# Two attention layers on one core: a chunk split in pairs, urgent score tiles on VectorE, and a new plan

## The chip, the cores and the metric

The kernel runs on one core of one Trainium2 chip. The metric is device time in microseconds (us). Runs of one kernel scatter over several us; the state of every run told here is "fast", and the slower ones among the fast runs of a kernel tend to have the lower granted TensorE clock (for the kernel before, 1082.2 us on average at 1.000 and 1086.3 at 0.994; more below). A ratio is the mean time of one kernel's fast runs over the mean of the other kernel's fast runs of the same rounds, so it is not quite the ratio of the medians that are quoted.

## The reference, cut to what matters

Twice in a row, an attention block and a gated MLP block over 2048 tokens of 448 values; 16 heads of 28.

```python
def _A_ref(x, wqkv, wo):                       # 16 heads, head size 28
    qkv = ...                                  # x @ wqkv, split
    scores = jnp.einsum("bhqd,bhkd->bhqk", q, k) * (Dh ** -0.5)
    p = _softmax(scores, axis=-1)
    o = jnp.einsum("bhqk,bhkd->bhqd", p, v)
    return ... @ wo
def _B_ref(x, w1, w2, w3, w4):
    h = _gelu(_layernorm(x, axis=-1) @ w1)
    hs = ... @ w2                              # h shifted by one and two tokens, quarter by quarter
    x1 = x + hs
    return x1 + _gelu(_layernorm(x1, axis=-1) @ w3) @ w4
x = A_x
for _ in range(2):                             # written out in the original
    x = x + _A_ref(_layernorm(x, axis=-1), A_wqkv, A_wo)
    x = x + _B_ref(_layernorm(x, axis=-1), B_w1, B_w2, B_w3, B_w4)
```

## The kernel before

A planner written in Python runs when the kernel is built. It sends the generators of all tasks through a model of the five engines and fixes the order of instructions on each engine; only that order and the semaphores reach the chip. Queries go in chunks of four tiles of 128 rows, keys in 16 tiles. ScalarE takes exp of three or two blocks of 512 scores at a time out of PSUM (`ps` in the profile, which the kernel uses in banks of 512 columns) into the buffers `PT`; TensorE multiplies them with V. Some score tiles are computed on VectorE instead (buffers `PD`), by an eviction (an instruction that reads the bank, after which the planner gives it free) and four steps:

```python
        def d_chain(blk, ys, pd):                 # a score tile on VectorE, after its eviction d_first
            ...
            yield op("dve", 0.6, lambda e: e.scalar_tensor_tensor(out=q, in0=lo, ..., in1=lo, ...), reads=[("yd", w)], writes=[fk])
            yield op("dve", 0.6, lambda e: e.scalar_tensor_tensor(out=q, in0=q, ..., in1=lo, ...), reads=[("yd", w), fk], writes=[fk])
            yield op(DTS[0], DTS[1], lambda e: e.tensor_scalar(out=pdt, in0=q, ...), reads=[fk], writes=[("pd", s)])
            ...
            yield op("dve", 0.6, lambda e: e.scalar_tensor_tensor(out=pdt.bitcast(I16), in0=hi, ...), reads=[("yd", w), ("pd", s)], writes=[("pd", s)])
```

TensorE is given fillers, matmuls on an identity into any PSUM bank that is free, meant to keep its clock up.

```python
    def keep_pe_busy(self, until):
        ...
            for b in banks:
                if b not in self.dead:
                    continue
                ds = self.P.deps("pe", reads, [key(b)])
                if all(d.t_end + 0.2 <= t + 0.02 for d in ds.values()):   # free by the PLAN's clock
                    pick = b
                    break
```

The softmax sums of a finished chunk go through two small DMAs with a reciprocal on VectorE between them:

```python
                yield dma("sp", lambda e: e.dma_start(out=rT[0:4 * n, :], in_=ub[28:128:32, ui, 0:NW]), ..., t=1.9, iss=0.57)
                yield op("dve", 0.86, lambda e: e.reciprocal(out=rT[0:4 * n, :], in_=rT[0:4 * n, :]), reads=[("rT",)], writes=[("rT",)])
```

## Time and profile before

| kernel before | us |
|---|---|
| three runs, median (lowest to highest) | 1083.24 (1082.53 to 1085.25) |
| the profiled execution | 1085.21 (span 1083.5, granted clock 0.997) |
| to the first exp / first to last exp / after it | 22.35 / 1006.20 / 54.95 |
| of the middle: ScalarE busy / idle | 989.62 / 16.58 |

The prediction shows the lines that these come from. One more group of the page belongs to them, the exps: count, busy time, mean ns, then the idle time just before them and its main releaser. (In the lines ACT is ScalarE, DVE VectorE, PE TensorE, PEld its weight loads, POOL GpSimd and SP SyncE; L1329 is line 1329 of the kernel.)

```profile
L1329 ACT ACTIVATE PT<-ps 128x1536 bf16<-128x1536 f32 (+1 forms) x808 | 925.0, 1337 | 16.7 <-PE ps L1182 8.7
```

808 exps make up 925 us of a span of 1083.5. Whatever shortens the kernel has to take exps away, or idle time before them, or shorten start and tail.

### The profile page before, as it was taken

The numbers are of one execution on the slowest core, as the hardware profiler recorded it, in microseconds if no ns is written. First come the engines' busy times: TensorE is split into PE (matmuls) and PEld (weight loads), VectorE is DVE, ScalarE is ACT, GpSimd is POOL, SyncE is SP. The second block draws the span as 40 slices with busy tenths as digits, with TensorE's granted clock in tenths as the row PEclk, the third lists the DMA queues.
The fourth block names the chain that finished last, engine by engine and source line by source line (L and its number), as shares of the span: only waits on it lengthen the run. The fifth ranks groups of instructions, "written<-read, shape, count | busy, mean of one in ns | idle before, by whom it ended". The sixth has DMA issues, their size and how long they took to land.

```text
span 1083.5 us, 34577 instructions
## 1 busy us (share of the span) xinstructions
PE 1012.5 (93%) x15675; PEld 415.0 (38%) x15675; DVE 608.5 (56%) x1180; ACT 1020.6 (94%) x921; POOL 311.8 (29%) x494
## 2 busy tenths in 40 slices
PE   7999999889999999999998999898999999999998
PEld 3333443334333432234333433343333333444455
DVE  7866156984663226841778544464866714365342
ACT  5999999999999999999997999999999999999942
POOL 3243106401541024510354000102763300333121
PEclk9999999999999999999998999999999999999999
DMA  4547202102301042000311032414221110211000
GB/s 123 123 119 224 76 21 51 28 12 74 68 21 22 26 106 48 20 17 25 100 41 31 27 114 82 115 56 114 61 47 30 31 51 12 62 39 21 12 15 28
DMA packets 91847, 62.08 MB, mean 57 GB/s; under 512 B 64580, under 2 KB 81092, under 8 KB 91700
## 3 DMA queue, kind: packets, MB, share of 16 engines
q1 hardware_dynamic: 88324, 51.78, 18.5%
q0 software_dynamic: 3376, 8.09, 2.7%
q8 instruction: 123, 2.02, 0.8%
q14 instruction: 24, 0.20, 0.1%
HBM read 26.98 MB, written 15.71 MB: 39 GB/s over the span
## 4 chain that ended last, share of the span: by engine, by line
ACT 80%; PE 13%; DVE 5%; DMA 1%; issue 1%; POOL 0%; DVEq 0%; ACTq 0%
ACT PT L1329 73%; PE ps L731 8%; ACT h2T L1709 4%; PE ps L1182 3%; PE ps L722 2%; ACT fb L1583 1%; DMA rT<-ub 1%; ACT L1329 1%; ACT L1709 1%; DVE st L862 1%; DVE fb L1239 0%; PE ps L1750 0%; DVE yd L1223 0%; DVE xn L882 0%; DVE PD L1241 0%
## 5 line engine op out<-in xcount | busy, mean ns | idle before, releaser
L1329 ACT ACTIVATE PT<-ps 128x1536 bf16<-128x1536 f32 (+1 forms) x808 | 925.0, 1337 | 16.7 <-PE ps L1182 8.7
L1182 PE MATMUL ps<-qT,kT 32*128 32x512 bf16 (+1 forms) x2304 | 317.0, 361 | 34.0 <-ACT PT L1329 26.0
L722 PE MATMUL ps<-PT,vaug 128*32 128x512 bf16 (+1 forms) x2275 | 252.0, 361 | 0.5 <-DVE ub L1408 0.5
L1182 PEld LDWEIGHTS ps<-qT,kT 32*128 32x128 bf16 x2304 | 79.4, 91 | 316.1 <-ACT PT L1329 294.8
L1750 PE MATMUL ps<-ident 128*32 128x256 bf16 x3888 | 172.2, 276 | 8.0 <-DVE x1b L1640 2.2
L731 PE MATMUL ps<-xT,w 128*32 128x512 bf16 (+2 forms) x2240 | 172.3, 361 | 1.7 <-DVE hT L1563 0.8
L1750 PEld LDWEIGHTS ps<-ident 128*32 128x32 bf16 x3888 | 108.3, 97 | 41.2 <-issue 15.3
L1700 DVE CAST h2T<-ps 128x512 bf16<-128x512 f32 (+2 forms) x108 | 65.1, 603 | 80.1 <-PE ps L731 71.0
L731 PE MATMUL ps<-w,h2T 128*32 128x448 bf16 x1512 | 101.4, 355 | 9.0 <-ACT h2T L1709 8.9
L1434 POOL TENSOR_TENSOR otn<-ub,fb 128x512 bf16<-128x512 f32 (+1 forms) x31 | 38.7, 1247 | 240.4 <-DMA fb<-rscr 238.2
L722 PEld LDWEIGHTS ps<-PT,vaug 128*32 128x32 bf16 x2275 | 70.5, 94 | 94.0 <-issue 78.0
L731 PEld LDWEIGHTS ps<-xT,w 128*32 128x32 bf16 (+1 forms) x2240 | 61.2, 95 | 54.9 <-issue 27.5
L990 POOL TENSOR_TENSOR sq<-kT 128x512 bf16<-128x512 bf16 (+2 forms) x32 | 31.0, 970 | 91.7 <-DVE kT L1004 88.4
L731 PEld LDWEIGHTS ps<-w,h2T 128*32 128x32 bf16 x1512 | 39.5, 96 | 43.9 <-issue 14.7
L1581 POOL TENSOR_TENSOR fb<-hT 112x512 f32<-112x512 bf16 (+1 forms) x32 | 35.8, 1119 | 66.0 <-DVE hT L1563 62.9
L731 PE MATMUL ps<-xT,wq_pad 128*32 128x512 bf16 x512 | 44.9, 383 | 2.7 <-DVE qT L1037 1.3
L731 PE MATMUL ps<-xT,wk_pad 128*32 128x512 bf16 (+2 forms) x576 | 46.4, 362 | 0.0
L868 POOL TENSOR_SCALAR vpe<-mv 128x1 f32<-128x1 f32 (+2 forms) x21 | 5.1, 245 | 142.0 <-DVE mv L863 142.0
L731 PE MATMUL ps<-wv,xT 128*32 128x448 bf16 x512 | 44.0, 356 | 0.8 <-ACT vaug L1081 0.6
L1423 DVE RECIPROCAL rT<-rT 16x128 f32<-16x128 f32 (+1 forms) x31 | 29.1, 938 | 27.5 <-DMA rT<-ub 27.3
L1655 POOL TENSOR_TENSOR x_res<-x_res,x1b 128x448 f32<-128x448 f32 x32 | 38.9, 1218 | 17.2 <-DVE xn L882 17.2
L990 POOL TENSOR_TENSOR sq<-qT 128x512 bf16<-128x512 bf16 x28 | 30.0, 1075 | 40.4 <-DVE qT L1037 36.7
(155 smaller groups left out, 1080.8 us busy)
## 6 DMA issues: line engine op xcount, KB each, us to landing
fb<-rscr SPq DMA_DIRECT2D x28, 256.0 KB
uscr<-ub SPq DMA_DIRECT2D x24, 256.0 KB
ub<-uscr SPq DMA_DIRECT2D x24, 256.0 KB
xnd<-xn SPq DMA_DIRECT2D x28, 128.0 KB, 1.7
x_res<-in_A_x_dram POOLq DMA_DIRECT2D x16, 224.0 KB, 3.8
xd<-x_res SPq DMA_DIRECT2D x16, 224.0 KB, 2.5
x_res<-xd SPq DMA_DIRECT2D x16, 224.0 KB, 3.0
out_dram<-obf SPq DMA_DIRECT2D x16, 112.0 KB, 1.7
```

Of the source, the lines that this page charges most:

```text
L722: return lambda e: e.matmul(out=out, lhsT=lhsT, rhs=rhs, start=start, stop=stop, **kw)
L731: r.append(e.matmul(out=out[c:c + w, :], lhsT=lhsT[:, c:c + w], rhs=rhs, start=start, stop=stop, tile_position=(0, c)))
L990: return op("pool", 0.15 + NW * 0.0018, lambda e: e.tensor_tensor(out=sq[:, si, 0:NW], in0=src, in1=src, op=ALU.mult), reads=rk, writes=[( ...
L1182: yield op("pe", max(0.055, 0.22 / nc_ * NW / 512.0), lambda e, i=i, kc=kc, j=j, g=g, a=a, NW=NW, bank=bank: e.matmul(out=ps[:, bank, i * ...
L1329: yield op("act", 0.05 + n * w * 0.000833, lambda e, bk=bk, s0=s0, n=n, w=w: e.activation(out=PT[:, s0:s0 + n, 0:w], in_=ps[:, bk[0]:bk[0] ...
L1423: yield op("dve", 0.86, lambda e: e.reciprocal(out=rT[0:4 * n, :], in_=rT[0:4 * n, :]), reads=[("rT",)], writes=[("rT",)])
L1434: yield op("pool", 0.2 + NW * 0.0021, lambda e: e.tensor_tensor(out=otn[:, g, 0:NW], in0=u, in1=rb[:, 0:NW], op=ALU.mult), reads=[uk, fk], ...
L1581: yield op("pool", 0.2 + NW * 0.00165, lambda e: e.tensor_tensor(out=f, in0=z, in1=z, op=ALU.mult), reads=hk, writes=[fk])
L1655: yield op("pool", 1.2, lambda e: e.tensor_tensor(out=X, in0=X, in1=X1, op=ALU.add), reads=[xk, ("x1b", s)], writes=[xk], deps=[nop_])
L1700: ev = op("dve", c_ps(NW), lambda e, fch=fch, b=b: e.tensor_copy(out=hb[:, fch, 0:NW], in_=ps[:, bi(b), 0:NW]), reads=[("ps", bi(b))], wri ...
L1709: yield op("act", c_act(nl * NW), lambda e: e.activation(out=hb[:, 0:nl, 0:NW], in_=hb[:, 0:nl, 0:NW], func=ACT.Gelu_apprx_tanh), reads=al ...
L1750: return [e.matmul(out=ps[32 * c:32 * c + 32, bi(b), 0:256].rearrange("p (a n) -> p a n", n=128), lhsT=ident[:, 32 * c:32 * c + 32], rhs=i ...
```

## The change

Its intent: let the first layer's last query chunk run as two pairs of tiles, so that its MLP starts sooner; compute more score tiles on VectorE in all chunks; raise the priority of such a tile's steps when its use is near; transpose the last keys of layer 1 straight from SBUF instead of through DRAM; order the tasks by one rank list; keep fillers longer off a bank that VectorE is to free (0.7 us for 0.2); and let the planner make a new plan from all this. The diff, cut to its core (the planner's bookkeeping is made faster in it too, and its search constants are new):

```diff
-    CHUNKS = {0: [(0, 4), (4, 4), (8, 4), (12, 4)], 1: [(0, 4), (4, 4), (8, 4), (12, 2), (14, 2)]}
+CHUNKS = {0: [(0, 4), (4, 4), (8, 4), (12, 2), (14, 2)], 1: [(0, 4), (4, 4), (8, 4), (12, 2), (14, 2)]}
+RANK = {k: round(1.1 + 0.05 * i, 3) for i, k in enumerate([('a', 0, 0), ('k', 0, 1), ...])}
-D_RATE = {(0, 0): 0, (0, 1): 0.06, (0, 2): 0, (0, 3): 0, (1, 0): 0.045, (1, 1): 0.03, (1, 2): 0.015}
+D_RATE = {(0, 0): 0.08, (0, 1): 0.05, (0, 2): 0.05, (0, 3): 0.13, (1, 0): 0.16, (1, 1): 0.1, (1, 2): 0.16}
+Sched.AGED = 0.1
 Sched.TARGET = 0.64
-Sched.LOW = 0.34
+Sched.LOW = 0
-Sched.DOUBT = {"dma": 0.8, "pool": 0.6, "dve": 0.2, "act": 0.1}
+Sched.DOUBT = {"dma": 1.0, "pool": 0.4, "dve": 0.05, "act": 0.2}
 ...
-                if all(d.t_end + 0.2 <= t + 0.02 for d in ds.values()):
+                if all(d.t_end + (0.7 if d.eng == "dve" else 0.2) <= t + 0.02 for d in ds.values()):
 ...
+            if kc_of(1, t) >= FASTKV:                   # FASTKV = 3: key tiles 11 to 15 of layer 1
+                xslot[t] = s
+                yield ("sig", ("xns", t))
 ...
         def d_chain(blk, ys, pd):
+            def urge():
+                return 1.0 if at[0] > si or (at[0] == si and at[1] >= kb - DURG) else DPRIO
-            yield op("dve", 0.6, lambda e: ..., reads=[("yd", w)], writes=[fk])
+            yield op(DST[0][0], DST[0][1], lambda e: ..., reads=[("yd", w)], writes=[fk], urge=urge)
 ...
-                if rate and CHUNKS[L][ch][1] == 4:
+                if rate and CHUNKS[L][ch][1] == 4 and SC.idle_share(8.0) >= FTH:
```

## The prediction

No term of the sum is among the cuts: it stands at 1083.2 - 5.0 + 0.3 - 11.1 + 1.5 = 1068.9. The GpSimd instruction beside the 1630 ns step (588.36 us) is an addition (L1655, 587.85 to 589.43 us).

> **What bounds the kernel now.** I began with the page's busy line, then asked for windows that cut the span at the first exp (22.35 us) and at the end of the last one (1028.55 us), with narrower ones where ScalarE had gaps. Columns: window, length, then busy time and count of PE, weight loads, VectorE, ScalarE and GpSimd, granted clock, DMA share, GB/s.
>
> ```profile
> PE 1012.5 (93%) x15675; PEld 415.0 (38%) x15675; DVE 608.5 (56%) x1180; ACT 1020.6 (94%) x921; POOL 311.8 (29%) x494
> ```
> ```profile
> 0.00:22.35 22.35, 14.45 (x215) 6.97 (x215) 16.75 (x66) 10.13 (x16) 9.58 (x19) 1.00 0.46 137
> ...
> 200.00:235.00 35.00, 30.09 (x483) 12.61 (x484) 29.05 (x49) 33.08 (x29) 9.01 (x10) 1.00 0.15 22
> 235.00:530.00 295.00, 279.45 (x4189) 105.44 (x4181) 149.51 (x264) 294.64 (x253) 85.15 (x136) 1.00 0.19 46
> ...
> 570.00:600.00 30.00, 26.39 (x392) 10.77 (x392) 25.02 (x54) 22.23 (x22) 13.20 (x16) 0.89 0.21 41
> 600.00:740.00 140.00, 131.65 (x2071) 57.24 (x2068) 69.94 (x144) 139.85 (x120) 12.42 (x20) 1.00 0.28 83
> 740.00:760.00 20.00, 17.26 (x252) 6.32 (x251) 10.15 (x15) 17.48 (x16) 5.10 (x5) 1.00 0.40 85
> ...
> 1028.55:1083.50 54.95, 50.68 (x990) 32.09 (x987) 18.81 (x37) 20.83 (x36) 9.43 (x21) 1.00 0.07 21
> ```
>
> The kernel is three pieces in a row: 22.35 us of start, 1006.2 us in which ScalarE is busy 989.6, and a tail of 54.95 in which PE is busy 50.7. ScalarE bounds the middle: from 235 to 530 us it is idle 0.36 us in all. PE looks as busy, but 172 us of it are the filler matmuls on `ident`[...]. The middle's 16.6 us of ScalarE idleness are concentrated: 7.8 at 570 to 600, 2.5 at 740 to 760, 1.9 each at 200 to 235 and at 530 to 535.3, 0.8 at 800 to 860, 1.7 elsewhere.
>
> The waits of ScalarE and VectorE's own order of time (start, duration, line and operation) say what the largest gap is:
>
> ```profile
> ACT PT L1329 <- PE ps L1182: 8.7, 18, 1.5
> ...
> ACT PT L1329 <- PE ps L722: 7.3, 2, 5.8
> ```
> ```profile
> 588.36 1.63 DVE L1237 SCALAR_TENSOR_TENSOR fb<-yd 128x512 f32<-128x512 uint16 x1
> 589.91 0.41 DVE L1241 TENSOR_SCALAR PD<-fb 128x512 bf16<-128x512 f32 x1
> 590.25 0.67 DVE L1640 SCALAR_TENSOR_TENSOR x1b<-x_res,mst,ps 128x448 f32<-128x448 f32 x1
> ...
> 592.00 0.66 DVE L1244 SCALAR_TENSOR_TENSOR PD<-yd,PD 128x512 int16<-128x512 int16 x1
> ```
>
> L722 is the product with V. Two waits of ScalarE end with it, 7.3 us. Before the longer one, PE stands until VectorE finishes a score tile that VectorE was computing itself (PD, ready at 592.66); four other VectorE instructions were put ahead of its last step. PE takes its V products in order, the exp needs a P buffer that those free, and it restarts at 593.17. So VectorE, 56% busy over the span, stops ScalarE where it is crowded.
>
> [...] Here exps of 1536 and 1024 columns last 1548 and 1126 ns: 0.824 ns per column. [...] the L1237 step has a median of 687 ns and lasts 1630 beside a GpSimd product. [...] here a tile's 128 KB store to `xnd` lands in 1.7 us[...].
>
> **The change part by part.** I compared the instruction orders of the two programs.
>
> 1. *Score tiles on VectorE.* PD tiles go from 29 to 40: VectorE gains 11 chains, about 11 x 3.4 = 37.5 us busy (689+752+748+477+743 ns), while ScalarE has 2008 blocks of 512 columns left of 2019 (803 exps, not 808). The exps occupy 925.0 us for 2019 blocks, 0.458 us each; 11 less is **-5.0 us** on the bounding engine.
>
> 2. *Split of the last chunk.* An exp block of a two-tile chunk covers two key tiles, so it is still 512 columns and the exp count does not rise. Six 256-wide score matmuls took 0.32 us, as three 512-wide did. V products become 512 of 256 columns for 256 of 512, at about 0.045 and 0.055 us: +9 us on PE, beside a stretch of some 117 us in which the old order holds roughly 14 us of fillers. On ScalarE, four tanh of 512 become eight of 256; from start to start they take 0.52 and 0.30 us: 8 x 0.30 - 4 x 0.52 = **+0.3 us**. Table switches stay seven pairs. The gain sought is that the first 12 to 13 tiles reach their MLP sooner and the crowd at the layer boundary is spread.
>
> 3. *Urgent score chains.* They ran at lowest priority; now a chain rises when the scores come within one key block of it. That aims at the two L722 waits (7.3 us) and partly at the score waits around 214 to 220. From the order of VectorE's instructions, with durations from the rows, I summed the work between evictions of successive V accumulators. Before, one 28-block segment of layer 1 (12.8 us of exp) carries 19.5 us of VectorE work: the 585 us stall. In the new order the fullest 28-block segment there carries 11.5 us, the fullest 64-block one 26.1 in 29.3. No segment after the start is overfull[...].
>
> 4. *Keys straight from SBUF.* For key tiles 11 to 15 of layer 1 a store (1.7 us) and a transposed load (5.1) give way to a transpose of 2.5: 4.3 us less latency. But from 600 to 740 us, where those keys are made, ScalarE idles 0.15 us. Directly worth **0**; it moves the point of need, nothing more.
>
> 5. *New plan* (rank list, larger allowances for DMA latency, no forced fillers). It may remove the 2.5 us at 740 to 760, where the chain runs through the DMA of the reciprocal into the output projection ahead of score matmuls. It may also bring waits of its own. Of the old 16.6 us I let 5.5 remain: some 7 of the 7.3 and 4 of the other 9.3 go, **-11.1 us**. This is judgement, the term I trust least.
>
> 6. *Start and tail.* First exps follow nearly the same work, one more V eviction on an idle ScalarE: 0. After the last scores, the new tail has 56 plain 256-wide matmuls for 40 (20 took 2.34 us: +1.9) and 40 col-tiled 512-wide for 56 (40 took 2.33: -0.9). Between the last V product and the output projection stand only fillers where before there was real work, but it is made up later: +0.5. **+1.5 us**.
>
> Sum: 1083.2 - 5.0 + 0.3 - 11.1 + 1.5 = 1068.9; I say 1068.5.
>
> **The rivals.** (a) *VectorE becomes the bound.* For it: 37.5 us more there, eleven PD tiles crowded in layer 1's third chunk (24 us of chain beside other work)[...]. Against: 56% busy, no overfull segment, chains now urgent. If it wins, 10 to 16 us of idleness remain: 1073 to 1079. (b) *PE order becomes the bound at the boundary.* In windows of 32 blocks the new order, like the old, has a few holding 1 to 2 us more PE work than ScalarE work (around blocks 896 and 1120); equal in number and size to before, so perhaps 2 us: 1071. (c) *Only the smaller exp count counts*, because each removed stall uncovers one behind it: -5 + 0.3 + 1.5 and 1 or 2 us of stalls, 1078 to 1080. Against: ScalarE runs hundreds of microseconds without a gap, so a removed stall is not refilled by a second resource. (d) *Everything works*: no idleness in the middle, 1083.2 - 5.0 + 0.3 - 16.6 + 1.5 = 1063.4; to go below, the tail would have to shrink too, whose PE work of about 50 us bounds it.
>
> **Range and chances.** 2% faster is 1061.6 us, below (d): it needs every stall gone and a tail 2 us better than I count. I give that 0.07. Slower by 2% (1105) needs new waits of 35 us, 0.01. Range 1063 to 1077: from no stalls to rival (a).
>
> **What would show it.** Exps x803 and about 920 us of exp time; ScalarE busy in the middle near 985; the wait of exps on L722's successor below 1 us; idleness between first and last exp about 5.5 us; tail near 56.5. Wrong if the exps wait on V products again (a), if the score waits exceed 9 us (b), or if the last exp ends less than 8 us earlier.

## More of the kernel before

The experiments ran in four groups of rounds, each group on another chip, so versions of different groups are compared by their ratios to the kernel before.

A filler waits for the last reader of its bank: the page of the kernel before has 8.0 us of idle time in front of fillers (L1750), 2.2 of it for the eviction `x1b`.

## The result, and the profile after

| | before | after |
|---|---|---|
| median of 4 runs (lowest to highest) | 1082.88 (1082.15 to 1085.25) | 1080.91 (1080.21 to 1082.57) |
| ratio, 95% interval | | 0.998, 0.9961 to 1.0000 |
| profiled execution: time / span | 1085.21 / 1083.5 | 1080.76 / 1079.0 |
| start / middle / tail | 22.35 / 1006.20 / 54.95 | 21.83 / 1002.82 / 54.35 |
| middle: ScalarE busy / idle | 989.62 / 16.58 | 984.97 / 17.85 |

The time is 12.4 us above the prediction and outside its range. The interval reaches 1, so these four runs alone hardly show a gain; the control below does. First the page's busy line of the changed kernel and its row of exps; then the windows of the three pieces, with columns as in the prediction.

```profile
PE 1009.5 (94%) x16117; PEld 426.2 (39%) x16117; DVE 642.3 (60%) x1250; ACT 1016.7 (94%) x922; POOL 315.8 (29%) x503
...
L1367 ACT ACTIVATE PT<-ps 128x1536 bf16<-128x1536 f32 (+1 forms) x803 | 918.8, 1338 | 17.6 <-PE ps L1212 16.8
```
```profile
0.00:21.83 21.83, 13.80 (x215) 6.85 (x215) 16.80 (x66) 10.67 (x16) 9.58 (x19) 1.00 0.48 140
21.83:1024.65 1002.82, 944.75 (x14942) 388.10 (x14941) 606.88 (x1146) 984.97 (x869) 294.36 (x460) 0.99 0.23 58
1024.65:1079.00 54.35, 50.96 (x966) 31.25 (x961) 18.61 (x39) 21.07 (x37) 11.84 (x25) 1.00 0.10 26
```

The work on ScalarE shrank as foreseen: 803 exps, 984.97 us busy in the middle, 4.65 less. The idle time before the exps did not shrink: 17.6 us for 16.7. The releaser changed, though. The waits of ScalarE for the score matmuls and the V product, in the changed kernel:

```profile
ACT PT L1367 <- PE ps L1212: 16.8, 15, 3.9
```

The wait on the V product (7.3 us before) has no line any more. The wait for scores went from 8.7 us in 18 pieces of at most 1.5 to 16.8 us in 15 pieces of up to 3.9. Four windows hold 11.9 of the 17.85 us of idleness (ScalarE's busy time is the fourth one after the length; the three numbers at the end are granted clock, DMA share and GB/s):

```profile
102.00:116.00 14.00, 11.45 (x149) 4.09 (x152) 5.69 (x9) 10.94 (x10) 3.32 (x4) 0.88 0.69 230
331.00:345.00 14.00, 12.08 (x188) 5.24 (x180) 13.52 (x22) 11.63 (x11) 8.94 (x10) 0.88 0.19 46
560.00:576.00 16.00, 15.37 (x185) 6.19 (x181) 9.94 (x20) 12.11 (x13) 5.17 (x6) 1.00 0.44 107
807.00:822.00 15.00, 12.56 (x147) 3.56 (x136) 8.59 (x16) 12.44 (x12) 6.21 (x7) 0.89 0.18 28
```

That is 3.06, 2.37, 3.89 and 2.56 us; a fifth, at 765 to 772 us, holds 1.5. A sixth went unnoticed in the experiments:

```profile
32.18 2.37 ACT L1367 ACTIVATE PT<-ps 128x1536 bf16<-128x1536 f32 x2 [2.00 <-PE ps L1212]
```

The kernel before waits 0.48 us at this place (31.18 us). The 2.0 us stand in every version of the changed kernel that was traced here, the repaired ones too, and their cause was not tested.

What ends each of the five, read in order of time (start, duration, engine, line, operation, and in brackets the idle time before it and its releaser):

The wait at 107 to 115 us:

```profile
102.25 0.71 SPq L1460 DMA_DIRECT2D rT<-ub  x1
...
108.62 0.94 DVE L1461 RECIPROCAL rT<-rT 16x128 f32<-16x128 f32 x1 [2.75 <-DMA rT<-ub]
109.49 0.62 DVE L1084 TENSOR_TENSOR qT<-qT,ps 128x512 bf16<-128x512 bf16 x1
...
110.17 1.03 PE L1783 MATMUL ps<-ident 128*32 128x256 bf16 x16 [2.17 <-DVE qT L1084]
...
111.78 1.45 ACT L1367 ACTIVATE PT<-ps 128x1536 bf16<-128x1536 f32 x1 [2.51 <-PE ps L1212]
```

No exp needs this reciprocal. But the eviction of a PSUM bank (L1084) stands behind it on VectorE: the matmuls that it reads ended at 106.42 us, and it started at 109.49, as the reciprocal ended. A filler on TensorE waited 2.17 us for that eviction, and the score matmuls stand behind the filler. So an 8 KB transfer stops ScalarE through two queues (the experiments test this chain). It took 6.4 us from issue to the reciprocal. The same transfer later, with a DMA share of 0.02, takes 1.7:

```profile
724.57 0.55 SPq L1460 DMA_DIRECT2D rT<-ub  x1
...
726.31 0.94 DVE L1461 RECIPROCAL rT<-rT 16x128 f32<-16x128 f32 x1 [1.77 <-DMA rT<-ub]
```

From 100 to 109 us the DMA engines were full with two weight loads that GpSimd had just issued, as the DMA view of that stretch says (packets, MB and share of the engines' time; then KB and us to landing of the larger load):

```profile
q0 software_dynamic: 534, 2.85, 97.3%
...
w<-in_B_w_dram POOLq DMA_DIRECT2D x1, 1568.0 KB, 12.0
```

This kind of wait is not new. In the kernel before, a reciprocal starts at 752.22 us after 5.63 us of waiting for the same kind of transfer, evictions of `qT` stand behind it, and ScalarE loses 1.48 us just after. There the transfer took 5.8 us with a DMA share of 0.38 and no such weight load. So a late reciprocal is seen with full engines (97.3%) and without them; what delays the transfer was not tested.

The wait at 337 to 344 us has another cause and the same last link, a filler:

```profile
337.05 1.64 DVE L1281 SCALAR_TENSOR_TENSOR PD<-yd,PD 128x512 int16<-128x512 int16 x1
338.61 1.26 DVE L1673 SCALAR_TENSOR_TENSOR x1b<-x_res,mst,ps 128x448 f32<-128x448 f32 x2
339.34 1.47 PE L1783 MATMUL ps<-ident 128*32 128x256 bf16 x24 [1.84 <-DVE x1b L1673]
...
341.40 1.45 ACT L1367 ACTIVATE PT<-ps 128x1536 bf16<-128x1536 f32 x1 [2.12 <-PE ps L1212]
```

The last step of a score tile on VectorE takes 1.64 us beside a GpSimd product (L1472, 336.69 to 338.14 us) instead of 0.69 (the median of its 40), and the eviction `x1b` stands behind it. At 814 to 820 us the w3 projection stands ahead of score matmuls and waits for its transposed input, issued at 809.88:

```profile
809.88 1.22 SPq L901 DMA_TRANSPOSE xT<-xn  x1
...
815.75 0.51 PE L745 MATMUL ps<-xT,w 128*32 128x384 bf16 x8 [1.77 <-DMA xT<-xn]
```

At 765 to 772 us it is the w1 projection in the same way. At 569 us no engine waits for a DMA at the time: TensorE is busy, with the q projections of layer 1's second chunk, which the next scores need.

### The profile page after: what moved, and what is told of

The parts are those of the page before. It is cut to its first block, busy times and chain, and to the rows that moved or that the text cites. A ratio compares the mean times of both kernels' runs of the same rounds, so it can differ in the third digit from the quotient of the medians.

```text
span 1079.0 us, 35560 instructions
## 1 busy us (share of the span) xinstructions
PE 1009.5 (94%) x16117; PEld 426.2 (39%) x16117; DVE 642.3 (60%) x1250; ACT 1016.7 (94%) x922; POOL 315.8 (29%) x503
## 4 chain that ended last, share of the span: by engine, by line
ACT 72%; PE 18%; DVE 6%; DMA 3%; issue 1%; POOL 1%; SPq 0%; DVEq 0%; ACTq 0%
ACT PT L1367 65%; PE ps L745 9%; PE ps L1212 4%; PE ps L736 4%; ACT h2T L1742 3%; ACT fb L1616 1%; DMA rT<-ub 1%; PE ps L1783 1%; ACT L1742 1%; DMA xT<-xn 1%; ACT L1367 1%; DVE st L876 1%; DMA fb<-rscr 0%; DVE rT L1461 0%; DVE hT L1596 0%
## 5 line engine op out<-in xcount | busy, mean ns | idle before, releaser
L1367 ACT ACTIVATE PT<-ps 128x1536 bf16<-128x1536 f32 (+1 forms) x803 | 918.8, 1338 | 17.6 <-PE ps L1212 16.8
L736 PE MATMUL ps<-PT,vaug 128*32 128x512 bf16 (+1 forms) x2520 | 250.7, 341 | 0.2 <-DVE ub L1446 0.2
L745 PE MATMUL ps<-xT,w 128*32 128x512 bf16 (+2 forms) x2176 | 165.0, 362 | 5.3 <-DMA xT<-xn 3.2
L1783 PEld LDWEIGHTS ps<-ident 128*32 128x32 bf16 x3860 | 110.7, 97 | 38.0 <-issue 13.2
L736 PEld LDWEIGHTS ps<-PT,vaug 128*32 128x32 bf16 x2520 | 74.8, 95 | 92.8 <-issue 79.3
L1472 POOL TENSOR_TENSOR otn<-ub,fb 128x512 bf16<-128x512 f32 (+1 forms) x36 | 42.1, 1169 | 150.8 <-DMA fb<-rscr 150.5
L1614 POOL TENSOR_TENSOR fb<-hT 112x512 f32<-112x512 bf16 (+1 forms) x36 | 38.6, 1074 | 71.6 <-DVE hT L1596 54.7
L745 PE MATMUL ps<-xT,wk_pad 128*32 128x512 bf16 (+2 forms) x576 | 48.8, 359 | 0.4 <-DVE qT L1058 0.4
L1461 DVE RECIPROCAL rT<-rT 16x128 f32<-16x128 f32 (+1 forms) x36 | 33.6, 934 | 22.2 <-DMA rT<-ub 22.1
L1253 DVE TENSOR_SCALAR yd<-ps 128x512 int32<-128x512 f32 x40 | 27.2, 685 | 31.4 <-PE ps L1212 30.8
L745 PE MATMUL ps<-wv,xT 128*32 128x448 bf16 x512 | 41.2, 356 | 1.2 <-DVE kmaxc L1036 0.8
```

The costliest lines, as they stand in the source:

```text
L736: return lambda e: e.matmul(out=out, lhsT=lhsT, rhs=rhs, start=start, stop=stop, **kw)
L745: r.append(e.matmul(out=out[c:c + w, :], lhsT=lhsT[:, c:c + w], rhs=rhs, start=start, stop=stop, tile_position=(0, c)))
L1367: yield op("act", 0.06 + n * w * 0.000833, lambda e, bk=bk, s0=s0, n=n, w=w: e.activation(out=PT[:, s0:s0 + n, 0:w], in_=ps[:, bk[0]:bk[0] ...
L1472: yield op("pool", 0.2 + NW * 0.0021, lambda e: e.tensor_tensor(out=otn[:, g, 0:NW], in0=u, in1=rb[:, 0:NW], op=ALU.mult), reads=[uk, fk], ...
L1614: yield op("pool", 0.2 + NW * 0.00165, lambda e: e.tensor_tensor(out=f, in0=z, in1=z, op=ALU.mult), reads=hk, writes=[fk])
L1783: return [e.matmul(out=ps[32 * c:32 * c + 32, bi(b), 0:256].rearrange("p (a n) -> p a n", n=128), lhsT=ident[:, 32 * c:32 * c + 32], rhs=i ...
```

## The experiments

The theory, called "own waits" in the expectations: the new order took the old waits away, and brought about five of its own; each has its own cause and gives its time back when mended. Rivals: "refill" (a second resource bounds the middle, and a removed wait opens another), too many tiles on VectorE, the split, and the luck of the plan.

Most experiments edit the finished order and nothing else (some also drop fillers): no task planned anew, no wait taken away. A helper records each instruction's function, reads and writes, moves the listed ones, and then derives all semaphores anew from reads and writes in the new order, so that a moved instruction still waits for what it needs. The numbers are positions in the plan.

```diff
+    def rearranged(self, moves, drops):
+        order = [op for i, op in enumerate(self.all) if i not in drops]
+        ...                                   # take out the listed ops, put them before or after a given one
+        Q, new = Plan(), {}
+        for op in order:
+            eng, fn, reads, writes, deps, dma, t_end = op.args
+            new[id(op)] = q = Q.add(eng, fn, reads, writes, [new[id(d)] for d in deps], dma, t_end)
+        return Q
 ...
         est = SC.run()
+        P = P.rearranged(MOVES, DROPS)
         P.finalize(nc, st)
```

**Control.** `MOVES = []`, `DROPS = []` on the changed kernel.

> A control for the repairs: the changed kernel with its order taken apart and put together again by the same helper, with nothing moved and nothing dropped. All theories: the changed kernel's time, 1079.5 to 1082.5 us, ratio to the kernel before 0.996 to 1.000, and its five waits in their places (about 3 us at 107 to 115, 2.4 at 337 to 344, 3.9 at 569, 1.5 at 766 to 771, 2.5 at 814 to 820). If it is faster than 1077 by itself, the repairs prove nothing.

Measured: 1081.25 us (1080.12 to 1083.08), ratio 0.9974 (0.9960 to 0.9989). The helper does nothing by itself, and the changed kernel's gain over the kernel before is about 3 us on this chip. In its profile the waits stand at 110 (3.1 us), 340 (2.4) and 569 (3.9); those at 768 and 815 are 4.3 and 1.2 here instead of 1.5 and 2.6, so these two waits vary from execution to execution.

**The reciprocal alone.**

```diff
+MOVES = [([1007, 1013], 'after', 1016)]     # reciprocal and its store behind two qT evictions
```

> The changed kernel with one repair: at 102 us the reciprocal that waits for its DMA, and the store of its result, go behind the next two VectorE instructions of the q projection; nothing else moves. Theory 'own waits' (the new order has some five waits of its own, each with its own cause, and each gives its time back when mended): ScalarE's 3.06 us of idleness from 107 to 115 us falls below 0.8, and the time is 1080.9 - 2.5 = about 1078.4. Rival 'refill' (some second resource bounds the middle, a removed wait opens another): the wait at 107 to 115 goes but the time stays within 0.7 us of 1080.9, with the idleness found later. Rival 'the DMA itself': the exps depend on that reciprocal, and the wait stays at about 3 us in place.

Measured: 1077.40 us (1074.57 to 1079.27), ratio 0.9941 (0.9923 to 0.9960), which by ratio is 3.6 us below the control (0.0033 of 1084; the control is of another group of rounds, on another chip). The window that lost 3.06 us, in this run:

```profile
102.00:116.00 14.00, 13.42 (x206) 5.60 (x207) 8.21 (x13) 14.00 (x14) 3.40 (x4) 1.00 0.70 232
```

ScalarE is busy 14.00 of 14.00, and the clock in it is 1.00 instead of 0.88. The DMA is as busy as it was (0.70 for 0.69); only nothing stands behind it any more. The rival "the DMA itself" falls. Not all of the 3.6 us need be this repair: in the same profile the wait at 340 is 1.3 us, with nothing moved there.

**Two others alone**, `x1b` and w3:

```diff
+MOVES = [([3231], 'after', 3246), ([3227], 'after', 3237),   # x1b evictions ahead of the tile's last two steps
+         ([8206, 8207, 8211], 'before', 8225)]               # w3 matmuls behind two rounds of scores
```

> Two of the four repairs alone: the evictions of x1b ahead of the score tile's last steps at 331 to 338 us, and the w3 projection behind score matmuls at 812 us; the reciprocal at 102 us and the order at 768 us stay as in the changed kernel. Theory 'own waits': only the waits at 337 to 344 and 814 to 820 go, 2.4 + 2.5 us, and the others stay: 1080.9 - 4.5 = about 1076.5. Rival 'the first wait sets all' (mending the reciprocal shifted everything after it, and the other repairs gave nothing): 1080 or more.

Measured: 1076.45 us (1075.30 to 1077.44), ratio 0.9927 (0.9912 to 0.9941): as expected, and by ratio 5.1 us below the control of the same rounds. The idleness at 340 and 815 is gone from the profile; the waits at 110 (3.1 us by its window) and 569 (3.9) are still there.

**All four**, with the w1 projection at 768 us:

```diff
+MOVES = [([1007, 1013], 'after', 1016), ([3231], 'after', 3246), ([3227], 'after', 3237),
+         ([7784, 7785, 7789, 7794, 7795], 'after', 7801),    # a w1 group behind scores
+         ([8206, 8207, 8211], 'before', 8225)]
```

> The changed kernel with four repairs of the order: the reciprocal at 102 us; at 331 to 338 us two evictions (x1b) ahead of the last two steps of a VectorE score tile; at 768 us the w1 projection behind the score matmuls; at 812 us the w3 projection behind them. Theory 'own waits': 3.06 + 2.37 + 1.45 + 2.56 = 9.4 us of ScalarE idleness are aimed at, 7.5 to 9 come back: 1072 to 1073.5, idleness of the middle 9 to 10 us instead of 17.9. Rival 'refill': above 1078. Rival 'too many VectorE tiles': the wait at 337 to 344 stays, since VectorE is overfull there, and only some 6 us come back, about 1075.

Measured: **1072.46 us** (1071.72 to 1073.04), ratio 0.9898 (0.9882 to 0.9914). This version beats both kernels (the changed one by ratio, across groups of rounds). Its waits for scores, and its middle:

```profile
ACT PT L1387 <- PE ps L1232: 9.3, 9, 3.9
```
```profile
21.90:1016.47 994.57, 940.18 (x14940) 387.49 (x14941) 606.40 (x1146) 984.15 (x869) 293.73 (x460) 1.00 0.23 58
```

Idleness of the middle 10.4 us instead of 17.85, with the same work on ScalarE. So three of the new waits were separable, and neither "refill" nor "too many tiles" explains them. The fourth repair gave nothing: the wait at 768 us is 1.6 us here, for the next w1 group now stood ahead of the scores and waited for the eviction that I had moved back. What is left besides is mainly the 3.9 us at 569 and the 2.0 at 32.

**The old waits, mended in the kernel before.** Were the 7.3 us that the change removed worth 7.3 us?

```diff
+MOVES = [([4909], 'after', 4875), ([4914, 4916, ..., 4928], 'after', 4903),    # tile's last step, V products
+         ([5446, 5453], 'after', 5438), ([5476, ..., 5491], 'after', 5444), ([5501, 5503, 5504], 'before', 5492)]
+DROPS = [5456, ..., 5471]                                                      # 16 fillers
```

> The kernel before with its two waits for a VectorE score tile mended by order alone: the last step of the tile goes ahead of other VectorE work at 531 and at 589 us, the V products go ahead on TensorE, and 16 fillers in between are dropped. No score tile more, no split. If the waits that the change removed are worth what I put them at, 5 to 7 us come back from 1083: 1076 to 1078, ratio about 0.994 to 0.995, and the two waits of exps on the V product fall from 7.3 to below 1.5 us. Rival 'refill': 1081 or more, the idleness reappearing within the next 30 us as waits for scores.

Measured: 1084.79 us (1083.64 to 1086.84), ratio 1.0013 (0.9998 to 1.0027): nothing came back. The waits on the V product fell from 7.3 to 1.6 us, and those for scores rose from 8.7 to 11.8. In order of time:

```profile
592.09 1.23 DVE L1261 TENSOR_SCALAR PD<-fb 128x512 bf16<-128x512 f32 x1
...
593.50 0.68 DVE L1428 COPY ub<-ps 128x512 f32<-128x512 f32 x1
...
594.24 0.80 PE L742 MATMUL ps<-PT,vaug 128*32 128x512 bf16 x6 [2.71 <-DVE ub L1428]
...
595.62 1.02 ACT L1349 ACTIVATE PT<-ps 128x1024 bf16<-128x1024 f32 x1 [3.53 <-PE ps L1202]
```

VectorE, busy 9.83 of the 10 us from 585 to 595, now holds up the eviction of the V accumulator (`ub`) instead of the score tile. A second try put that eviction ahead of two more steps of a tile:

```diff
+         ([5475, 5490], 'after', 5498)])
```

> The earlier repair of the kernel before gave nothing back (1084.8 for 1083.9): the wait for the VectorE tile at 589 us turned into a wait for the eviction of the V accumulator, VectorE being busy 9.8 of the 10 us from 585 to 595. Here that eviction goes ahead of two more steps of a score tile too. Theory 'VectorE is overfull there': a third wait follows, and at most 2 us come back, 1082 to 1084. Rival 'only the order was wrong': 5 us come back, 1078 to 1079.

Measured: 1084.21 us (1080.80 to 1086.97), ratio 1.0002 (0.9980 to 1.0024). The profiled execution was the fastest of its four, with 5.7 us of idleness left between 580 and 600. Here "refill" fits: in the old kernel VectorE is overfull for some 10 us, and both orders tried only moved the wait about. In the changed kernel work has left that stretch: VectorE is busy 20.65 us from 570 to 600, for 25.02 before.

**The wait at 569 us.** The q projections there need tile 7, stored 20 us earlier by the plan; their load waits for one of two `xT` buffers, which the w1 projection of tiles 12 and 13 holds from 520 to 550 us of the plan.

```diff
+         ([5766, 5772, 5779, 5789], 'after', 5727), ([5799], 'after', 5729),    # last w1 quarter earlier
+         ([5796], 'after', 5728),                                               # then the load
+         ([q projections..., w3 groups...], 'refill', None),                    # q first in the slots of both
+         ([7805], 'after', 7808)]
+DROPS = [5855, 5856, 5857, 5862]
```

> The four repairs plus two: the last quarter of the w1 projection of the tiles 12 and 13 goes ahead on TensorE (it held one of the two xT buffers from 520 to 550 us of the plan, so that the load for layer 1's second q projection waited), that load and its four q projections go ahead of the w3 projection, whole groups swapped, four fillers dropped; and at 768 us one more w1 group goes behind the score matmuls. Theory 'own waits, the one at 569 us caused by a buffer that the split's small chunk holds': the 3.9 us at 569 fall below 1, and about 0.7 more at 768: 1072.5 - 4 = 1068 to 1069, idleness of the middle about 7.5 us. Rival 'refill' (TensorE is full at the layer boundary, the w3 projection and the later keys come late in turn): above 1071, with waits for scores between 575 and 620.

Measured: 1074.58 us (1073.28 to 1078.92), ratio 0.9910 (0.9891 to 0.9929): not below the four repairs, where 1068 to 1069 was expected. The wait is still 3.6 us; the load came 5.0 us earlier (554.96 and 549.94 us in the two traces, 6.0 counted from the first exp), but the scores stood behind the w3 groups that I had put after the q projections. So once more, with those groups moved behind the scores, one at a time:

```diff
+         ([5809, 5810, 5813, 5814, 5819], 'after', 5915), ([5816, ..., 5823], 'after', 5926),
+         ([5828, ..., 5836], 'after', 5938), ([5845, ..., 5854], 'after', 5945)]
```

> As the run with the two more repairs, but the four w3 groups that gave way to the q projections now go behind the first score matmuls of the new chunk, one group at a time between later score matmuls, instead of ahead of them. Before this run: [...] the wait at 565 us was still 3.6 us, TensorE busy 5.0 of every 5 us from 540 to 565 with no filler to give way. Theory 'only the order': the wait falls below 1.5 us and the time is 1070 to 1071.5. Rival 'TensorE is full at the boundary' (it has some 5 us of fillers in the 120 us from 530 to 650): the w3 groups push the later work, the same 3 us come back as waits for scores between 570 and 620, and the time stays at 1072.5 to 1074.5.

Measured: 1075.87 us (1074.53 to 1079.69), ratio 0.9926 (0.9906 to 0.9947), above what either theory expected. Two windows of its profile:

```profile
565.00:570.00 5.00, 3.83 (x43) 1.35 (x36) 2.72 (x6) 3.97 (x4) 1.51 (x2) 1.00 0.16 56
570.00:575.00 5.00, 3.75 (x30) 1.76 (x29) 2.51 (x6) 2.70 (x4) 0.00 (x0) 1.00 0.53 105
```

The 3.9 us are now 5.3 in several pieces from 560 to 580. My theory of the held buffer falls as the sole cause. But "TensorE is full" isn't shown either: it is busy 3.8 of 5 us in these windows, waiting about half a microsecond at a time, mostly for VectorE to evict the w3 groups' results (`h2T`). What bounds this boundary stays open; I found no order that mends it.

**Single parts of the change**, planned anew, so each of these also draws a new plan, and one of them shows how far a draw alone can move the time:

```diff
-FASTKV = 3
+FASTKV = 9                       # keys never straight from SBUF
```

> The changed kernel without the keys transposed straight from SBUF (all keys by the store and the transposed load, as before); the planner then makes nearly the same plan (same 803 exps, 40 VectorE tiles, same lateness of the q projection at 569 us). My prediction put this part at 0: within 1.5 us of the changed kernel, 1079.4 to 1082.4. If the fast keys are what brought the waits at 768 and 814 us (more transposes on the queue), the run is 2 to 4 us faster than the changed kernel; if they saved time, 2 us or more slower.

Measured: 1084.54 us (1079.59 to 1089.09), ratio 1.0009 (0.9986 to 1.0032). Above the 1079.4 to 1082.4 that I expected and some 3 us slower by ratio than the changed kernel, as foreseen for the case that the part saves time; but the six runs spread over 9.5 us (granted clock 0.997 in the fastest, 0.991 in the slowest). The waits at 110, 340, 569 and 815 are all in its profile, so the fast keys did not bring them. Whether the part is worth 3 us, or this plan only has more places where TensorE's clock falls (it is 0.66 from 1020 to 1035 us in the profile, which is of the slowest run), isn't settled.

```diff
-CHUNKS = {0: [(0, 4), (4, 4), (8, 4), (12, 2), (14, 2)], ...
+CHUNKS = {0: [(0, 4), (4, 4), (8, 4), (12, 4)], ...      # and ORDER and BGROUPS to match
```

> The changed kernel with its first layer's last chunk left whole (four tiles), everything else of the change kept; the planner then makes 50 VectorE tiles and 799 exps. If the split is what brought the wait at 569 us (a small chunk holding an xT buffer), that wait is gone here. What the split was meant for should show in its place: the keys of layer 1's last tiles, or another product of the last chunk's MLP, come late, and one wait of 10 to 22 us appears between 660 and 720. Expected 1083 to 1093, slower than the changed kernel by 2 to 12 us; if the split is worth nothing, 1076 or less, since 4 exps fewer are worth 4 us.

Measured: 1095.27 us (1094.47 to 1100.38), ratio 1.0105 (1.0082 to 1.0129), 799 exps: slower, and 2 us beyond what was expected. The wait at 569 us is gone, and this stands in its place:

```profile
712.72 3.71 ACT L1367 ACTIVATE PT<-ps 128x1536 bf16<-128x1536 f32 x3 [20.95 <-PE ps L1212]
```

TensorE finishes the last tiles' w4 products at 697 us and makes the last keys from 706 us on. So in this plan the keys come late without the split, and with the split comes the wait at 569. This is one plan, though: the kernel before has no split in its first layer and no wait of this size, and the next experiment moves the time further by a planner constant alone.

```diff
-Sched.TARGET = 0.64
+Sched.TARGET = 0.65              # share of TensorE time that fillers aim at
```

> The changed kernel with one constant of the planner moved by a hair: the share of TensorE time that fillers aim at, 0.65 for 0.64. Nothing of the change is undone: same split, same 40 VectorE tiles, same 803 exps, same urgency. If the parts of the change set the time, this stays within 2 us of 1081. If the luck of the plan does (theory 'own waits'), the time moves by 5 to 20 us, with a longer wait at the layer boundary for the q projection (the planner itself now leaves ScalarE about 17 and 5 us there instead of 4): 1086 to 1101.

Measured: 1107.82 us (1103.96 to 1114.00), ratio 1.0216 (1.0185 to 1.0248): by ratio some 26 us slower than the changed kernel with the same parts, and more than the 5 to 20 us expected. ScalarE stands 21 us between 568 and 590. The plan, not the parts, set this; how many waits a plan brings is in part luck.

```diff
-                return 1.0 if at[0] > si or (at[0] == si and at[1] >= kb - DURG) else DPRIO
+                return DPRIO
```

> The changed kernel with the score chains of VectorE at lowest priority throughout, as before the change; all else kept, planned anew (the plan then has 39 VectorE tiles, 804 exps, and a late q projection, about 17 us). If urgency is what took the waits for VectorE tiles away, the exps wait on the V product for 3 to 10 us again; if the spread of the load did it, this wait stays at 0 and only the late projection and a new plan's waits are seen. Time 1095 to 1115 either way, for the late projection.

Measured: 1108.32 us (1106.81 to 1114.26), ratio 1.0236 (1.0205 to 1.0268), with the late projection as expected, and this among the waits of ScalarE:

```profile
ACT PT L1367 <- PE ps L736: 10.2, 2, 5.2
```

L736 is the V product: the old kind of wait is back, at 813 and 819 us. Before the second, TensorE stands 1.09 us until VectorE finishes a score tile (`PD`). The four other plans traced with urgency (the changed kernel, and those without fast keys, without the split and with 0.65) have no such wait. This speaks for the urgency, though the waits are at other places than the old ones. What took away the wait at 593, the urgency or the lighter stretch around it, was not separated.

## Why the prediction was wrong

Point by point, in the prediction's own order:

1. *Score tiles on VectorE, -5.0 us, and tanh, +0.3.* Right in sum: ScalarE's busy time in the middle fell by 4.65, for -4.7 foretold. That it fits so closely is luck, for the exps fell by 6.2 (925.0 to 918.8) and the rest of ScalarE's work there rose by 1.5. VectorE gained 33.8 us where 37.5 were counted, and didn't become the bound.
2. *Urgent chains.* The effect is right: all 7.3 us of waiting on the V product are gone, and in a plan without the urgency such waits are back. The reading of the longer wait was too simple: in the trace TensorE did not stand until the tile was ready (592.66). It ran fillers, stood 1.17 us at a filler for the eviction `x1b` until 590.97, and the V products came behind this in its order. Only when they were moved ahead (in "The old waits, mended") did TensorE stand for the tile, 1.58 us.
3. *Keys from SBUF, 0.* Not settled.
4. *The new plan.* **The step that failed**: "Of the old 16.6 us I let 5.5 remain: some 7 of the 7.3 and 4 of the other 9.3 go, -11.1 us." Idleness rose to 17.85, so the term is +1.3 and not -11.1. What I said would go did go, and more: 1.7 us at 210, 1.9 at 530, the 7.8 from 570 to 600 and 2.1 of 2.5 at 740 to 760 by ten-microsecond windows, 13.5 in all. I had counted as if nothing came in: "It may also bring waits of its own" stands in the text with no number beside it. The repairs put numbers there. By the windows above, 3.06, 2.37, 3.89, 2.56 and 1.5 us, 13.4 in all, came in, and 1.5 more at 32 us: 14.9, which with the 13.5 gone makes the +1.3 to within 0.2. A reciprocal in front of an eviction while a 1.6 MB weight load runs, and projections in front of score matmuls while their transposed input is on its way, could have been looked for in the new order, which I had, and the old profile shows the first kind at 752 us; I only summed VectorE's and TensorE's work between two points. Such sums find overfull engines. They don't find one late instruction at the head of a queue.
5. *The tail, +1.5.* Measured -0.6; the start, 0, measured -0.5. Together they make the prediction 2.6 us too high, in the other direction.

The rest of the sum is the reference point. The two profiled spans differ by 4.5 us, the medians by 2.0: the profile of the kernel before is an execution of 1085.21 where its median is 1082.88. Over all rounds, runs of the kernel before with a granted clock of 1.000 took 1082.2 us on average (6 runs), with 0.998 1083.7 (14), with 0.997 1084.1 (5), with 0.995 1085.2 (11), with 0.994 1086.3 (5). All four runs of the changed kernel had 0.994 or 0.995, those with four repairs 0.998 to 1.000. This fits a cost of its own for each new wait: in the windows at 102, 331 and 807 us the granted clock was 0.88 to 0.89, and mended it is 1.00. TensorE had stood still there for 2.17, 1.84 and 1.77 us (with shorter gaps beside them), and each time a stretch of 3.4 us at a granted clock of 0.50 began near the end of the stand: at 110.2, 338.9 and 816.8 us, where TensorE resumed at 110.17, 339.34 and 815.75. Yet waits of 2.08 and 2.08 us (kernel before, until 368 and 505 us) and of 1.97 and 1.70 us (changed kernel, until 388 and 531 us) left the clock at 1.00, and a fourth such stretch, from 936.3 us, comes after waits of 1.10 and 0.91 us. So these traces give no length of wait that decides.

Two of the prediction's own signs of being wrong came: the waits for scores exceed 9 us (16.8), and the last exp ends 3.9 us earlier instead of 8 or more. The first was the sign of (b), TensorE's order at the layer boundary; that may hold for the wait at 569, which stays open, but at the others TensorE stood still (2.17, 1.84 and 1.77 us) instead of having too much to do. Of the rivals, (c) gave the time, 1078 to 1080, nearly. Its mechanism, "each removed stall uncovers one behind it", holds for the old kernel's boundary, where both mendings only moved the wait, and in part for the wait at 569. It doesn't hold for the three that the repairs removed: those lay some 60 us or more from the larger old ones, and when they went, the time came back.

## What to carry to other kernels

When an order is remade, count the waits that come in as carefully as those that go: look at every queue for an instruction that waits for a DMA or may run slowly beside a GpSimd product (1.64 us for 0.69 here), and ask what stands behind it, and what stands behind that. An instruction that nothing waits for (a filler, an early reciprocal, a projection for later) costs nothing only while it can't block: here fillers stood 2.17 and 1.84 us, and the exps behind them. A profile then names each such wait, and mending them by order alone, four small moves of which one gave nothing, brought more (0.9974 to 0.9898, 8 us) than the change did (2 to 3).
